# Chunked attention and a leaky-ReLU layer on one core: product 3 added onto product 5's bank, first-layer weight sums on VectorE, attention steps moved

## The chip, the cores and the metric

The kernel runs on one core of one Trainium2 chip. The metric is the device time of one execution in microseconds (us), lower is better. 0.5% of it (1.4 us) is about what a measurement of this kernel can tell from no change.

## The reference

```python
def _attn_ref(q, k, v):                       # q, k, v: (8, 8, 576, 64)
    chunk, scale = 64, 1.0 / np.sqrt(D)       # every head in 9 independent chunks of 64
    scores = scale * np.matmul(q_c, k_c.transpose(0, 1, 2, 4, 3))
    scores = scores - np.max(scores, axis=-1, keepdims=True)
    attn = np.exp(scores)
    attn = attn / (np.sum(attn, axis=-1, keepdims=True) + 1e-09)
    return np.matmul(attn, v_c)...

def _moe_ref(x, w_in, w_out):                 # x: (4608, 512), w_in: (512, 2048), w_out: (2048, 512)
    h = x @ w_in
    return np.maximum(0.01 * h, h) @ w_out
```

The attention output, transposed to (4608 tokens, 512), is the x of the second function. Inputs and output are float32; the kernel computes in fp16 with fp32 accumulation.

## The kernel before

**Tiling.** The 4608 tokens are 36 attention units u of 128 tokens, and 20 blocks j of the two layers: blocks 0 to 3 have 128 tokens, blocks 4 to 19 have 256. A unit's output lands in `xT` (model dimension on the partitions). A block needs the units of its tokens.

**Attention of a unit.** Step "dq"/"dk" transposes q and k on VectorE (`QZ`, `KT`; units below 14 use TensorE, "tq"/"tk"), "s" is the score matmul into `Sp`, "m"/"nb" the maximum and the scaled negative of it on VectorE, "f" the exponentials on ScalarE (`ex`, sums in `z`), "z" adds 1e-9 and inverts on VectorE (`ze`, `zi`), "n" scales on GpSimd (`en`, from unit 9 on), "d" transposes by DMA from SP's queue (`et`), "v" is the matmul with v (`xp`), and "a" the copy to `xT` on ScalarE.

**Layers.** The first layer of blocks 6 to 16 is "mm1": per chunk of the work list a 512-column bank `hT`, which "G" (`act1`) turns into `gT` through a leaky ReLU. The second layer of blocks 4 to 19 is a seven-product scheme (Strassen's in Winograd's form): products P1 to P7 of 8 matmuls each, whose operands are halves of `gT` and `w_outT`, sums of token halves `SG` ("sum", VectorE), and sums of weight halves `TW` ("W", VectorE). P1, P6, P7, P4 accumulate one after the other in bank X, and after each of the first three ScalarE copies it to `keep` ("combX"). P2, P5 and P3 are combined by VectorE with one of these copies into the output tile `osb` ("combW", "combZ"), and SP's queue stores it. In blocks 6 to 15, P3 accumulates in the same bank Z as P5, after P5's value was read by `combine(j, 5)`. In blocks 4, 5 and 16 to 19 (`ONE`), P2, P5 and P3 have a bank each, from a ring of four (`mm`), which `hT` uses too; there `combine(j, 0)`, one more VectorE add, puts P5 onto the copy that P3 is combined with.

**Wide blocks.** Blocks 17, 18 and 19 (`WIDE`) use the seven products in the first layer as well, for two halves s of the hidden units ("a" and "b" in the work list): `wide(j, s, n)` is product n, 8 matmuls of 128 columns. Products 1, 6, 7, 4 accumulate in `xbank`; "lx" (`wide_x`) copies it to `xkeep` on ScalarE. Products 2, 5, 3 go to `xpr` banks of the ring, and "la" (`wide_m`) adds such a bank onto copies on VectorE: product 5 onto the copies after 7 and after 6, product 3 onto that after 6. "lp" is the leaky ReLU on ScalarE. The token sums `xs` are made on VectorE, and the 16 weight sums `WS` (`w_in_sum`, a difference of two 128x512 fp16 tiles each) on GpSimd, 8 of them from w_inT alone and 8 that need another WS too.

**Order.** The order on every engine is written out by the program, in a work list (`chunks`) of TensorE work in fixed order. `now["step"]` counts it: 1 per chunk, 0.5 per wide product. Everything else is an event with a due step: the table of constants (`SPACE`, `VO`, `O_*`) gives the due steps of the attention units, loads and weight sums, and `later(D_*, ...)` those of copies and combinations, counted from the chunk that they follow. Before a chunk, all due events are issued. `flush` issues named ones at once. Each engine works its instructions in that order; waits come from the data and from buffers.

Of the kernel before, what the change touches and what calls it, by code (L numbers as in the profile page):

```python
# [16 lines left out]
def kernel(  # L17
# [178 lines left out]
    def product(j, n, i):  # L196
        one, two = rows(j)
        g, w = gT[j], w_outT
        where, left, right = {
            1: ("X", g[:, :HF, one], w[:, :HF, :HM]),  # L200
            2: ("W", g[:, HF:, one], w[:, HF:, :HM]),
            3: ("Z", SG.get((j, 4)), w[:, HF:, HM:]),
            4: ("X", g[:, HF:, two], TW.get(4)),
            5: ("Z", SG.get((j, 1)), TW.get(1)),
            6: ("X", SG.get((j, 2)), TW.get(2)),
            7: ("X", SG.get((j, 3)), TW.get(3)),
        }[n]
        if where != "X" and j in ONE:
            where = n
        if (j, where) not in bank:  # L210
            tag, bufs = {"X": ("qp", 1), "Z": ("kp", 1)}.get(where, ("mm", 4))
            if j in EARLY:
                tag, bufs = "mm", 4
            bank[j, where] = psp.tile([128, 2, HM], FP32, name=f"pr{where}", tag=tag, bufs=bufs)
        to = bank[j, where]
        for f in range(HF):
            nc.tensor.matmul(  # L217
                out=to[:, i, :],
                lhsT=left[:, f, i * 128:(i + 1) * 128],
                rhs=right[:, f, :],  # L220
                start=(j, where) not in opened,
                stop=(f == HF - 1),
                skip_group_check=True,
            )
            opened.add((j, where))

    def combine(j, n):
# [25 lines left out]
        if n == 4:  # L253
            nc.scalar.activation(out=to, in_=half(bank[j, "X"]), func=AFT.Copy, bias=0.0, scale=1.0)
        else:
            nc.vector.tensor_tensor(  # L256
                out=to,
                in0=half(bank[j, n if j in ONE else "W" if n == 2 else "Z"]),
                in1=half(kept[j, {2: 1, 5: 7, 3: 6}[n]]),
                op=ALU.add,  # L260
            )
# [61 lines left out]
    def w_in_sum(n, s, t):  # L323
# [14 lines left out]
        nc.gpsimd.tensor_tensor(out=WS[n, s, t], in0=x, in1=y, op=ALU.subtract)  # L338
# [16 lines left out]
    def wide(j, s, n):  # L355
# [14 lines left out]
        if n in (1, 6, 7, 4):  # L370
            if n == 1:
                XB[j, s] = psp.tile([128, 4, 128], FP32, name="xbank", tag="kp" if s or j == WIDE.start else "Sp", bufs=1)
            to = XB[j, s]
        else:
            to = XM[j, s, n] = psp.tile([128, 4, 128], FP32, name="xpr", tag="mm", bufs=4)
        for i in range(4):
            for t in range(2):
# [4 lines left out]
                    start=(n != 6 and n != 7 and n != 4 and t == 0 and (n != 1 or i == 0)),  # L382
# [21 lines left out]
    def wide_m(j, s, n):  # L404
        of = XM.pop((j, s, n))
        for m in {2: (1,), 5: (7, 6), 3: (6,)}[n]:
            to = XK[j, s, m]
            nc.vector.tensor_tensor(out=to, in0=of, in1=to, op=ALU.add)  # L408
            if (n, m) != (5, 6):
                later(D_P, "lp", j, s, n != 2, n == 5, to)  # L410

# [125 lines left out]
    def fill():  # L537
# [10 lines left out]
        elif kind == "wide":  # L548
# [4 lines left out]
            if p in (1, 6, 7, 4):  # L553
                flush("lx")
                if p == 6:
                    flush("xs")
            if p == 1 and a == 0:
# [7 lines left out]
            elif p != 5:  # L565
                flush("lx", "la")
# [9 lines left out]
        elif kind == "prod":  # L576
# [17 lines left out]
            if p == BLOCKS[j] // 256 - 1:  # L594
# [14 lines left out]
                elif j in ONE:  # L609
                    if a in (1, 6, 7, 4):  # L610
                        later(D_K, "combX", j, a)
                    else:
                        flush("combX", "combZ")
                        if a == 5:
                            later(D_C, "combZ", j, 0)
# [20 lines left out]
    D_S = 1.75  # L636
    D_K = 0
    D_C = 2.25
    D_U = 0.5
    D_T = 2.5  # L640
    D_H = 0
    D_I = 1.75
    D_P = 2.75
    O_S = 162
    O_B = 198
    O_A = 0.75
    XS_POOL = 0
    O_G = 168
    D_O = 1.5
    D_D = 2.5  # L650
# [224 lines left out]
    def zero_act(i):  # L875
# [49 lines left out]
    SPACE = [5.0, 4.5, 6.5, 4.5, 6.0, 4.5, 8.0, 4.5, 6.0, 6.0, 9.5, 6.5, 6.0, 7.0, 8.0, 5.5, 5.5, 10.5, 9.0, 6.5, 8.0, 9.5, 9.5, 5.0, 6.0, 8.5, 6.5, 9.5, 5.5, 10.5]  # L925
    VO = [1.0, 1.0, 1.0, -0.5, 3.0, -1.5, 4.0, 1.5, 0.5, -1.0, 1.0, -1.0, 2.5, 4.5, 5, 1.0, 1.0, 5.0, 3, 1.0, 6, 0.5, 1.5, 0.0, -1.5, -3.0, 3.0, 2, -2.0, -3.5]
    O_T = 4.0
    O_P = 3.5
    O_Q = 5.5
    O_R = 0.75  # L930
    O_M = 0
    O_X = 1.0
    O_F = 1.5
    O_H = 1.0
    O_Z = 6.5
    O_N = 3.0
# [41 lines left out]
    for b in range(3, B):  # L978
        for i in range(16):
            at(T[9 * b // 2 - 5] - (O_E if b == 3 else O_L) + i // 2 * D_D, "D", b, i)  # L980
# [52 lines left out]
```

## Time and profile before

| | |
|---|---|
| time, median of 3 runs | 287.69 us (287.49 to 288.5) |
| span of the profiled execution | 287.5 us |
| TensorE busy | 274.4 us, 95% |
| VectorE busy | 221.7 us, 77% |
| ScalarE busy | 205.4 us, 71% |
| GpSimd busy | 164.6 us, 57% |
| granted TensorE clock, mean | 0.994 |

The profiled execution's own time is its span of 287.5 us, 0.2 us below the median of the three runs; no other time is given for it. In the views, PE is TensorE's matmuls, PEld its weight loads, DVE is VectorE, ACT is ScalarE, POOL is GpSimd, SP the queue engine. A row of the timeline is start, length, engine, line, operation, output<-inputs, shapes, count, and in brackets the idle time before it with what ended it. A row of the windows is the stretch, its length, and then busy time and number of instructions of PE, PEld, DVE, ACT and POOL, the granted clock, the mean busy share of the DMA engines in a unit of one, and GB/s.

### The profile page before, as it was taken

How to read it: one execution, taken by the hardware profiler on the slowest of the kernel's cores; microseconds unless marked ns; L12 is line 12 of the kernel's file. 1: busy time of each engine (PE TensorE's matmuls, PEld its weight loads, DVE VectorE, ACT ScalarE, POOL GpSimd, SP SyncE). 2: the span in 40 equal slices, each digit the busy share in tenths (PEclk: the TensorE clock that was granted, in tenths of full speed). 3: DMA queues.
4: the chain of work that ended last, by engine and by line, in shares of the span. 5: the costliest groups of instructions: out<-in, count | busy, mean ns of one | idle time of the engine just before them, and what ended most of it. 6: DMA issues, size and time to landing. Idle time of an engine off the chain costs nothing.

```text
span 287.5 us, 8377 instructions
## 1 busy us (share of the span) xinstructions
PE 274.4 (95%) x3338; PEld 240.6 (84%) x3338; DVE 221.7 (77%) x434; ACT 205.4 (71%) x657; POOL 164.6 (57%) x187
## 2 busy tenths in 40 slices
PE   7888999999999999999999999998599998999995
PEld 4568946899999999999999999987489997999994
DVE  5866666998897869698869788679967768787683
ACT  6855724775658787898887888787477868777671
POOL 8747642987958775984599459719631196000000
PEclk9999999999999999999999999999799999999999
DMA  9999999999999999999899999929053304111113
GB/s 146 151 185 177 203 172 125 123 137 123 163 118 161 67 88 177 95 166 107 119 106 135 100 146 109 156 81 103 0 182 95 93 18 93 22 73 40 39 39 109
DMA packets 182647, 32.66 MB, mean 114 GB/s; under 512 B 173776, under 2 KB 178128, under 8 KB 182608
## 3 DMA queue, kind: packets, MB, share of 16 engines
q0 software_dynamic: 158880, 18.23, 116.2%
q1 hardware_dynamic: 22688, 13.64, 20.3%
q8 instruction: 26, 0.43, 0.6%
q10 hardware_dynamic: 1040, 0.26, 0.4%
q14 instruction: 13, 0.11, 0.2%
HBM read 36.96 MB, written 9.44 MB: 161 GB/s over the span
## 4 chain that ended last, share of the span: by engine, by line
PE 85%; DMA 6%; DVE 5%; POOL 2%; issue 1%; ACT 0%; ACTq 0%; DVEq 0%; POOLq 0%
PE hT L291 34%; PE prX L217 19%; DMA w_inT<-in_moe_w_in_dram 6%; PE prZ L217 6%; PE pr L217 5%; PE oP L418 5%; PE xbank L378 3%; PE prW L217 3%; DVE SG L194 3%; PE Sp L736 3%; PE xp L830 3%; PE xpr L378 2%; DVE xs L353 1%; POOL VB L113 1%; POOL k_in L92 1%
## 5 line engine op out<-in xcount | busy, mean ns | idle before, releaser
L291 PE MATMUL hT<-xT,w_inT 128*128 128x256 f16 (+1 forms) x1216 | 120.2, 251 | 4.8 <-DVE osb L256 4.1
L291 PEld LDWEIGHTS <-w_inT 128*128 128x128 f16 x1216 | 96.6, 98 | 13.4 <-DVE osb L256 4.3
L306 ACT ACTIVATE gT<-hT 128x512 f16<-128x512 f32 x120 | 71.1, 619 | 19.9 <-PE hT L291 19.8
L766 ACT ACTIVATE ex<-Sp,nb 128x64 f16<-128x64 f32 x176 | 53.0, 333 | 7.2 <-DVE nb L758 6.6
L797 POOL TENSOR_TENSOR en<-ex,zi 128x512 f16<-128x512 f16 x27 | 30.6, 1134 | 42.5 <-ACT keep L233 17.7
L217 PEld LDWEIGHTS <-SG 128*128 128x128 f16 x512 | 48.7, 98 | 5.3
L745 DVE TENSOR_REDUCE mx<-Sp 128x8 f32<-128x512 f32 x36 | 24.7, 686 | 21.3 <-PE Sp L736 20.9
L217 PEld LDWEIGHTS <-gT 128*128 128x128 f16 x384 | 37.0, 99 | 4.4
L766 ACT ACTIVATION_READ_ACCUMULATOR ex<-Sp,nb 128x1 f32 x176 | 40.0, 227 | 0.0
L106 POOL DMA_DIRECT2D q_d<-in_q_dram x40 | 33.5, 838 | 8.2 <-DVE QZ L718 8.1
L106 POOL DMA_DIRECT2D k_d<-in_k_dram x40 | 32.8, 820 | 2.0 <-DMA k_d<-in_k_dram 1.3
L217 PE MATMUL prX<-TW,SG 128*128 128x256 f16 x256 | 33.2, 273 | 0.0
L718 DVE STREAM_TRANSPOSE QZ<-q_d 64x512 f16<-64x512 f16 (+1 forms) x48 | 31.1, 653 | 0.5
L233 ACT ACTIVATE keep<-prX 128x256 f32<-128x256 f32 x48 | 19.1, 398 | 14.4 <-PE prX L217 14.3
L844 ACT ACTIVATE xT<-xp 128x512 f16<-128x512 f32 x36 | 22.3, 618 | 7.3 <-PE xp L830 7.1
L113 POOL DMA_DIRECT2D VB<-in_v_dram x16 | 18.6, 1173 | 13.7 <-PE xp L830 11.0
L194 DVE TENSOR_TENSOR SG<-gT 128x1024 f16<-128x1024 f16 x32 | 23.3, 728 | 3.9 <-ACT gT L306 3.6
L408 DVE TENSOR_TENSOR xkeep<-xpr,xkeep 128x512 f32<-128x512 f32 x24 | 15.7, 683 | 6.7 <-ACT xkeep L402 4.3
L217 PE MATMUL prX<-TW,gT 128*128 128x256 f16 x128 | 17.5, 282 | 0.0
L194 DVE TENSOR_TENSOR SG<-gT,SG 128x1024 f16<-128x1024 f16 x16 | 16.7, 1045 | 0.1
L217 PE MATMUL prX<-w_outT,gT 128*128 128x256 f16 x128 | 16.6, 273 | 0.0
L726 DVE STREAM_TRANSPOSE KT<-k_d 128x512 f16<-128x512 f16 (+1 forms) x24 | 15.6, 655 | 0.4
(88 smaller groups left out, 428.0 us busy)
## 6 DMA issues: line engine op xcount, KB each, us to landing
out_dram<-osb SPq DMA_DIRECT2D x35, 256.0 KB, 3.1
VB<-in_v_dram POOLq DMA_DIRECT2D x16, 288.0 KB, 6.3
q_d<-in_q_dram POOLq DMA_DIRECT2D x40, 72.0 KB, 4.5
k_d<-in_k_dram POOLq DMA_DIRECT2D x40, 72.0 KB, 4.6
w_inT<-in_moe_w_in_dram POOLq DMA_DIRECT2D x8, 256.0 KB, 8.3
w_outT<-in_moe_w_out_dram POOLq DMA_DIRECT2D x4, 512.0 KB, 12.1
q_in<-in_q_dram POOLq DMA_DIRECT2D x11, 128.0 KB, 7.9
k_in<-in_k_dram POOLq DMA_DIRECT2D x11, 128.0 KB, 7.8
```

Source lines behind the costliest of these rows:

```text
L106: nc.gpsimd.dma_start(out=t[p0:p0 + 32, m, :, :, :].rearrange("p h b d -> p (h b) d"), in_=src[b, h0:h0 + 2, :, dh * 32:dh * 32 + 32].rear ...
L113: nc.gpsimd.dma_start(out=VB[b % NVB][m * CH:(m + 1) * CH, :, :, m * CH:(m + 1) * CH].rearrange("p h c d -> p (h c) d"), in_=v[b, m * H // ...
L194: nc.vector.tensor_tensor(out=SG[j, n], in0=x, in1=y, op=op)
L217: nc.tensor.matmul(out=to[:, i, :], lhsT=left[:, f, i * 128:(i + 1) * 128], rhs=right[:, f, :], start=(j, where) not in opened, stop=(f == ...
L233: nc.scalar.activation(out=half(kept[j, n]), in_=half(bank[j, "X"]), func=AFT.Copy, bias=0.0, scale=1.0)
L291: nc.tensor.matmul(out=hT[:, i, :], lhsT=w_inT[:, t, fc * 128:(fc + 1) * 128], rhs=xT[:, t, r0:r0 + tb], start=(t == 0), stop=(t == NT - 1),)
L306: nc.scalar.activation(out=gT[j][:, nf * a:nf * a + nf, c0:c0 + tb], in_=HT.pop((j, a, p)), func=AFT.Prelu, bias=0.0, scale=1.0, alpha=0.01,)
L718: nc.vector.transpose(out=qz[s * CH:(s + 1) * CH, :, e0:e0 + n, s, :], in_=flat(qkd[b][0])[s * CH:(s + 1) * CH, :, at:at + n * CH].rearran ...
L745: nc.vector.tensor_reduce(out=MX[u], in_=SP[u], axis=AXL.X, op=ALU.max)
L766: nc.scalar.activation(out=E[u][:, i, :], in_=SP[u][:, i, :], func=AFT.Exp, bias=NB[u][:, i:i + 1], scale=SCL, accum_out=Z[u][:, i:i + 1],)
L797: (nc.gpsimd if u >= UP else nc.vector).tensor_tensor(out=E[u], in0=ex, in1=ZI.pop(u).unsqueeze(2).to_broadcast((128, 8, CH)), op=ALU.mult)
L844: nc.scalar.activation(out=xT[:, :, at:at + G], in_=xp, func=AFT.Copy, bias=0.0, scale=1.0)
```

## The change

1. `SOLO` (blocks 4, 5 and 19) takes the place of `ONE` for the question of who has a bank for each product. In blocks 16, 17 and 18, P2 gets bank W, and P3 accumulates in P5's bank Z, both still from the ring of four; `combine(j, 0)` is gone there, and before P3 all pending combinations are flushed, so that P5's value is read first.
2. In the wide blocks, product 3 accumulates in product 5's `xpr` bank, which is kept for it; the second add of product 5 (onto the copy after 6) is gone. Before products 2 and 3 the pending "lx" and "la" are now flushed ahead of the matmuls, no longer behind them.
3. `w_in_sum` runs on VectorE instead of GpSimd.
4. Numbers of the tables move: attention units are issued up to 2 steps earlier or later (`SPACE`), their "v" up to 4 steps (`VO`), the loads of q and k for units from 14 on are spread over more steps, combinations are due one step later (`D_C`), "la" one step earlier (`D_I`), and the weight sums 1 step apart instead of 0.75. The work list is the same, chunk by chunk.

```diff
+    SOLO = EARLY + (LAST,)
...
-        if where != "X" and j in ONE:
+        if where != "X" and j in SOLO:
             where = n
         if (j, where) not in bank:
-            tag, bufs = {"X": ("qp", 1), "Z": ("kp", 1)}.get(where, ("mm", 4))
+            tag, bufs = {"X": ("qp", 1), "Z": ("mm", 4) if j in ONE else ("kp", 1)}.get(where, ("mm", 4))
...
-                in0=half(bank[j, n if j in ONE else "W" if n == 2 else "Z"]),
+                in0=half(bank[j, n if j in SOLO else "W" if n == 2 else "Z"]),
...
-        nc.gpsimd.tensor_tensor(out=WS[n, s, t], in0=x, in1=y, op=ALU.subtract)
+        nc.vector.tensor_tensor(out=WS[n, s, t], in0=x, in1=y, op=ALU.subtract)
...
+        elif n == 3:
+            to = XM[j, s, 3] = XM.pop((j, s, -5))
         else:
             to = XM[j, s, n] = psp.tile([128, 4, 128], FP32, name="xpr", tag="mm", bufs=4)
...
-                    start=(n != 6 and n != 7 and n != 4 and t == 0 and (n != 1 or i == 0)),
+                    start=(n in (1, 2, 5) and t == 0 and i == 0),
...
-        for m in {2: (1,), 5: (7, 6), 3: (6,)}[n]:
-            to = XK[j, s, m]
-            nc.vector.tensor_tensor(out=to, in0=of, in1=to, op=ALU.add)
-            if (n, m) != (5, 6):
-                later(D_P, "lp", j, s, n != 2, n == 5, to)
+        if n == 5:
+            XM[j, s, -5] = of
+        to = XK[j, s, {2: 1, 5: 7, 3: 6}[n]]
+        nc.vector.tensor_tensor(out=to, in0=of, in1=to, op=ALU.add)
+        later(D_P, "lp", j, s, n != 2, n == 5, to)
...
+            elif p != 5:
+                flush("lx", "la")
...
             elif p != 5:
-                flush("lx", "la")
                 later(D_I, "la", j, a, p)
...
+            if a == 3 and j not in SOLO:
+                flush("combX", "combZ")
...
-                        if a == 5:
-                            later(D_C, "combZ", j, 0)
...
-    D_C = 2.25
+    D_C = 3.25
...
-    D_I = 1.75
+    D_I = 0.75
...
-    VO = [1.0, 1.0, 1.0, -0.5, 3.0, -1.5, 4.0, 1.5, 0.5, -1.0, 1.0, -1.0, 2.5, 4.5, 5, 1.0, 1.0, 5.0, 3, 1.0, 6, 0.5, 1.5, 0.0, -1.5, -3.0, 3.0, 2, -2.0, -3.5]
+    VO = [0.5, 1.5, 1, -1, 3, -1.5, 3.5, 0, -2, 2, 3, 2, 1, 4.5, 8, 4.5, 4.5, 2, 3.5, -1, 6, 0.5, -1, -0.5, -2, -4, 3, 5, -5, -3.5]
```

Where instructions stand on an engine, before and after, at the three places that matter below. Lines after the change are one to four higher. The numbers behind `WS_` and `osb_` tell buffers apart.

GpSimd, from the last load of v (`VB`) to the end, before (the eight WS from w_inT, with `en` of the units between):

```order
L113 DMA VB_64<-in_v_dram 64x36x64 x2
L338 TENSOR_TENSOR WS_3912<-w_inT 128x512
L338 TENSOR_TENSOR WS_3927<-w_inT 128x512
L338 TENSOR_TENSOR WS_3943<-w_inT 128x512
L338 TENSOR_TENSOR WS_3954<-w_inT 128x512
L338 TENSOR_TENSOR WS_3957<-w_inT 128x512
L338 TENSOR_TENSOR WS_3982<-w_inT 128x512
L338 TENSOR_TENSOR WS_3998<-w_inT 128x512
L797 TENSOR_TENSOR en<-ex,zi 128x512
L338 TENSOR_TENSOR WS_4025<-w_inT 128x512
L797 TENSOR_TENSOR en<-ex,zi 128x512 x4
```

and after, from two `en` ahead of that load to the last instruction of the queue's work:

```order
L801 TENSOR_TENSOR en<-ex,zi 128x512
L107 DMA q_d<-in_q_dram 32x36x32
L107 DMA k_d<-in_k_dram 32x36x32
L801 TENSOR_TENSOR en<-ex,zi 128x512
L114 DMA VB_64<-in_v_dram 64x36x64 x2
L801 TENSOR_TENSOR en<-ex,zi 128x512 x7
```

Nothing but `en` is left on GpSimd behind the last load.

VectorE, around the token sums 3 and 4 (`SG`) of block 13, before:

```order
L194 TENSOR_TENSOR SG<-gT 128x1024
L718 STREAM_TRANSPOSE QZ_65<-q_d 64x8x64
L726 STREAM_TRANSPOSE KT<-k_d 128x512
L194 TENSOR_TENSOR SG<-gT,SG 128x1024
L256 TENSOR_TENSOR osb_3925<-prW,keep 128x256
L745 TENSOR_REDUCE mx<-Sp 128x8
L758 TENSOR_SCALAR nb<-mx 128x8
```

and after:

```order
L195 TENSOR_TENSOR SG<-gT 128x1024
L195 TENSOR_TENSOR SG<-gT,SG 128x1024
L339 TENSOR_TENSOR WS_3921<-w_inT 128x512
L257 TENSOR_TENSOR osb_3943<-prW,keep 128x256
L339 TENSOR_TENSOR WS_3945<-w_inT 128x512
L339 TENSOR_TENSOR WS_3957<-w_inT 128x512
L794 TENSOR_SCALAR ze<-z 128x8
L796 RECIPROCAL zi<-ze 128x8
L749 TENSOR_REDUCE mx<-Sp 128x8
L762 TENSOR_SCALAR nb<-mx 128x8
```

The weight sums stand between the instructions that free P2's bank (`osb<-prW`) and that start the next unit's softmax (`mx`, `nb`).

VectorE, in the first wide block (17), from the token sum 2 of block 16 to the adds of wide products 5 and 3, before (the `xkeep x3` are two adds of product 5 and one of product 3):

```order
L194 TENSOR_TENSOR SG<-SG,gT 128x1024
L353 TENSOR_TENSOR xs<-xT 128x256
L353 TENSOR_TENSOR xs<-xT,xs 128x256
L790 TENSOR_SCALAR ze<-z 128x8
L792 RECIPROCAL zi<-ze 128x8
L408 TENSOR_TENSOR xkeep<-xpr,xkeep 128x512
L194 TENSOR_TENSOR SG<-gT 128x1024
L256 TENSOR_TENSOR osb_4733<-pr_4673,keep 128x256
L194 TENSOR_TENSOR SG<-gT,SG 128x1024
L408 TENSOR_TENSOR xkeep<-xpr,xkeep 128x512 x3
```

and after:

```order
L195 TENSOR_TENSOR SG<-SG,gT 128x1024
L412 TENSOR_TENSOR xkeep<-xpr,xkeep 128x512
L794 TENSOR_SCALAR ze<-z 128x8
L796 RECIPROCAL zi<-ze 128x8
L195 TENSOR_TENSOR SG<-gT 128x1024
L195 TENSOR_TENSOR SG<-gT,SG 128x1024
L412 TENSOR_TENSOR xkeep<-xpr,xkeep 128x512
L257 TENSOR_TENSOR osb_4756<-prW,keep 128x256
L412 TENSOR_TENSOR xkeep<-xpr,xkeep 128x512 x2
```

The first single `xkeep` is the add of product 2; the second is now the only add of product 5, which product 3's matmuls wait for, and it stands behind both remaining token sums.

More of the change, by code (lines that the diff above doesn't have):

```diff
@@ L635 @@
     D_G = 0.5
-    D_S = 1.75
+    D_S = 2
     D_K = 0
-    D_C = 2.25
-    D_U = 0.5
+    D_C = 3.25
+    D_U = 0.25
     D_T = 2.5
     D_H = 0
-    D_I = 1.75
[L643 to L646, printed above, removed]
+    D_I = 0.75
+    D_P = 3.5
+    O_S = 162.75
+    O_B = 197
+    O_A = 1
     XS_POOL = 0
-    O_G = 168
-    D_O = 1.5
-    D_D = 2.5
+    O_G = 151.5
+    D_O = 0.5
+    D_D = 3.25
     UP = 9
@@ L977 @@
         at(T[u - 3] - O_D, "g", u)
-    for b in range(3, B):
+    for b in range(B2, B):
         for i in range(16):
-            at(T[9 * b // 2 - 5] - (O_E if b == 3 else O_L) + i // 2 * D_D, "D", b, i)
+            t0, dt = (D_0, D_1) if b == 2 else (T[9 * b // 2 - 5] - (O_E if b == 3 else O_L), D_D)
+            at(t0 + i // 2 * dt, "D", b, i)
     for n in range(4):
```

35 lines of the change are left out of this document (19 added, 16 removed), and 12 rows, old and new, of the table FRONT.

## The prediction

> **What bounds the kernel now.** I read the page's head first, then the windows, then the waits and the timeline of the two places where TensorE is not busy. The page: busy time of the engines, and the granted clock in 40 slices of 7.2 us.
>
> ```profile
> PE 274.4 (95%) x3338; PEld 240.6 (84%) x3338; DVE 221.7 (77%) x434; ACT 205.4 (71%) x657; POOL 164.6 (57%) x187
> PEclk9999999999999999999999999999799999999999
> ```
>
> TensorE is the bound, and in one slice, the 29th (201 to 208 us), its clock was cut. The windows say how full the rest is (stretch, then PE, PEld, DVE, ACT, POOL busy, clock, DMA, GB/s):
>
> ```profile
> 60.00:70.00 10.00, 10.00 (x141) 9.32 (x139) 9.72 (x20) 5.17 (x11) 7.29 (x10) 1.00 3.18 124
> ...
> 150.00:160.00 10.00, 10.00 (x112) 9.04 (x110) 8.88 (x17) 8.09 (x35) 7.61 (x9) 1.00 2.63 146
> 160.00:170.00 10.00, 10.00 (x112) 9.03 (x110) 8.18 (x16) 8.39 (x35) 4.98 (x5) 1.00 1.24 129
> ...
> 180.00:190.00 10.00, 10.00 (x106) 9.01 (x105) 7.12 (x14) 7.96 (x33) 4.79 (x6) 1.00 1.80 111
> ...
> 200.00:205.00 5.00, 0.94 (x10) 0.62 (x8) 4.97 (x5) 0.38 (x1) 4.93 (x5) 1.00 0.46 32
> 205.00:210.00 5.00, 5.00 (x33) 3.86 (x31) 2.81 (x10) 4.15 (x20) 2.15 (x2) 0.66 0.06 11
> ...
> 241.00:246.00 5.00, 4.11 (x61) 3.73 (x60) 4.86 (x11) 3.18 (x8) 2.37 (x3) 1.00 0.46 74
> ...
> 250.00:260.00 10.00, 10.00 (x152) 9.61 (x150) 7.32 (x16) 7.55 (x16) 0.00 (x0) 1.00 0.14 54
> ```
>
> From 60 us to 200 us and from 250 us on TensorE has no gap, at full clock: an engine that gets faster there gives nothing, and one that gets later costs only if it eats its slack. Two holes are left: 4.06 us idle at 200 (5.00 - 0.94), followed by 5 us at a clock of 0.66, which is 0.34 x 5.00 = 1.7 us lost; and 0.89 us idle at 241 to 246, at full clock. The work list up to the first 44 us is the same in both, so its gaps stay. The floor for this amount of TensorE work is therefore 287.5 - 4.06 - 1.7 - 0.89 = 280.85 us.
>
> What makes the first hole, in the timeline (start, length, engine, line):
>
> ```profile
> 196.66 8.26 POOL L338 TENSOR_TENSOR WS<-w_inT 128x512 f16<-128x512 f16 x7
> ...
> 197.67 6.25 DVE L194 TENSOR_TENSOR SG<-gT,SG 128x1024 f16<-128x1024 f16 x1
> ...
> 199.21 1.04 PE L217 MATMUL prX<-TW,SG 128*128 128x256 f16 x8
> ...
> 203.84 0.41 DVE L256 TENSOR_TENSOR osb<-prW,keep 128x256 f32<-128x256 f32 x1
> ...
> 204.31 2.63 PE L291 MATMUL hT<-xT,w_inT 128*128 128x256 f16 x16 [4.06 <-DVE osb L256]
> ```
>
> ```profile
> L194 DVE TENSOR_TENSOR SG<-gT,SG 128x1024 f16<-128x1024 f16 x9 | 6.5, 718 | 0.0
> ```
>
> The token sum of block 13 that takes 0.72 us elsewhere (nine between 60 and 195 us, second fence) took 6.25 us, exactly while GpSimd ran seven weight sums back to back. Behind it in VectorE's queue stood `osb<-prW`, which frees P2's bank of the ring of four; `hT` needed that bank, and TensorE stood for 4.06 us. The second hole, in the first wide block:
>
> ```profile
> 240.07 1.25 DVE L353 TENSOR_TENSOR xs<-xT 128x256 f16<-128x256 f16 x1
> 241.35 1.12 DVE L353 TENSOR_TENSOR xs<-xs,xT 128x256 f16<-128x256 f16 x1
> ...
> 243.00 0.28 DVE L353 TENSOR_TENSOR xs<-xT 128x256 f16<-128x256 f16 x1
> ...
> 244.38 1.22 DVE L194 TENSOR_TENSOR SG<-gT 128x1024 f16<-128x1024 f16 x1
> ```
>
> ```profile
> 241.13 1.20 POOL L338 TENSOR_TENSOR WS<-w_inT,WS 128x512 f16<-128x512 f16 x1
> 241.32 0.69 ACT L402 ACTIVATE xkeep<-xbank 128x512 f32<-128x512 f32 x1
> 242.62 0.61 PE L378 MATMUL xbank<-xs,WS 128*128 128x128 f16 x8 [0.65 <-ACT xT L844]
> 244.00 1.04 POOL L797 TENSOR_TENSOR en<-ex,zi 128x512 f16<-128x512 f16 x1 [1.68 <-ACT xkeep L402]
> 244.56 0.60 ACT L402 ACTIVATE xkeep<-xbank 128x512 f32<-128x512 f32 x1 [0.69 <-PE xbank L378]
> 245.23 0.61 PE L378 MATMUL xpr<-xs,w_inT 128*128 128x128 f16 x8
> ```
>
> Again two sums (`xs`) took 1.1 to 1.25 us beside a GpSimd weight sum and 0.28 us after it, and the wide product 6 at 242.62 waited for the second. So both holes come from VectorE instructions with two SBUF inputs that stood still while GpSimd did arithmetic.
>
> **The change, part by part.** (1) Weight sums off GpSimd. It loses 16 instructions, and behind the last v load only `en` is left there, each 1 us long and apart from the next. Both holes lose their cause: 4.06 + 1.7 = 5.8 us at 200. At 241 the gain is less than the hole: product 6 also needs the copy of `xbank` that ended at 242.01 (241.32 + 0.69), so it starts at about 242.1 instead of 242.62, 0.5 us.
>
> A rule of the Trainium skill bears on this, in "SBUF — State Buffer", section "Who interferes with whom": a VectorE instruction with two SBUF inputs and a GpSimd instruction that reads SBUF exclude each other, and the second to start waits until the first has finished. This trace agrees that they exclude each other, but not on the length: the sum stood through the starts of several of GpSimd's, not through one. By the rule's letter the wait would be one weight sum; what that would make of the time is the third rival.
>
> (2) The same 16 on VectorE. No row has this form there. `xs` (256 elements) takes 0.28 us, a free `SG` (1024) 0.72 us; between them 512 elements are about 0.42 us (an estimate, linear between the two), 16 x 0.42 = 6.7 us, 3.4 us for each eight. Ends: 16 x 0.28 = 4.5 and 16 x 0.72 = 11.5 us. The first eight fall into one period of a block, 16 steps or about 14.5 us. In the windows 150 to 170 VectorE is idle 20.00 - 17.06 = 2.9 of 20 us, so 2.1 in 14.5: the eight put it up to 1.3 us behind, which the next period gives back. Who waits for that: `osb<-prW` stands behind one weight sum only; what is late is the token sum 1 of the next block, which P5 needs. The prices, from the chain and from VectorE's timeline and groups:
>
> ```profile
> 193.44 0.87 PE prW L217 x8
> 194.31 0.25 PE Sp L736 x8
> ```
>
> ```profile
> 194.58 0.69 DVE L745 TENSOR_REDUCE mx<-Sp 128x8 f32<-128x512 f32 x1 [0.49 <-PE Sp L736]
> 195.31 0.38 DVE L758 TENSOR_SCALAR nb<-mx 128x8 f32<-128x8 f32 x1
> ...
> 196.29 0.71 DVE L718 STREAM_TRANSPOSE QZ<-q_d 64x512 f16<-64x512 f16 x1
> ```
>
> ```profile
> L790 DVE TENSOR_SCALAR ze<-z 128x8 f32<-128x8 f32 x36 | 9.1, 254 | 2.4 <-ACT ex L766 1.7
> L792 DVE RECIPROCAL zi<-ze 128x8 f32<-128x8 f32 x36 | 7.3, 203 | 3.0
> ```
>
> Between the score matmul that VectorE answers first in that period and this P5 lie 5 chunks of 0.87 us and two attention steps of 0.25 us, 4.85 us. VectorE needs 0.69 + 0.38 + 0.25 + 0.20 + 3 x 0.71 (transposes) + 0.72 (the sum) = 4.4 us ahead of P5. So 0.45 us of the 1.3 are covered, and the cost is 0 to 0.9 us; I take 0.2, near the low end, because instructions start up to 0.1 us before the one ahead has ended in the timeline, and a sum held by a weight sum no longer occurs. The second eight fall where the list of transposes ends (unit 35 is the last) and VectorE waits for score matmuls: 0.
>
> (3) Removed adds.
>
> ```profile
> L408 DVE TENSOR_TENSOR xkeep<-xpr,xkeep 128x512 f32<-128x512 f32 x24 | 15.7, 683 | 6.7 <-ACT xkeep L402 4.3 <-PE xpr L378 2.3
> L237 DVE TENSOR_TENSOR keep<-pr,keep 128x256 f32<-128x256 f32 x6 | 2.5, 410 | 0.3 <-ACT xT L844 0.3
> ```
>
> Six of 0.683 us and three of 0.410 us, 5.3 us of VectorE, all behind 244 us, where TensorE has no gap from 250 us on (the row above): worth 0.
>
> (4) The new waits: product 3 now waits until VectorE has read product 5's bank. In blocks 18 and 19 the list puts b7, P7, P5, a4, b4, P4 (3.9 us) between a7 and a3, and a4, b4, P4, a3, b3 between P5 and P3; the chain (copy 0.6, add 0.68, some 0.2 us for each handover) is under 2 us: hidden. In block 17, b7 to b3 has P3 and b4 between, 1.3 us, about as long as the chain: 0 to 0.1. But a7 to a3 has only P6 and one "v", 1.1 us. From the rows: the copy after a7 ends at 244.56 + 0.60 = 245.16, the add cannot end before 245.85, and without other delay a3 would start at 245.23, or 245.46 with the "v" of unit 34, which now stands ahead of it: a wait of 0.4 us at least. Two token sums stand ahead of the add, and `en` at 244.00 still holds one of them (the 1.22 us row): two times 0.68 and 1.04 after 243.87 is 246.3, the add ends at 247.0, a wait of 1.5 us. I take 1.0, in the middle, as the order of SG and `en` decides.
>
> (5) Moved steps. Of the units' "v", those with the smallest room between the landing of `et` and "v" decide. The tightest is unit 9:
>
> ```profile
> 73.40 1.20 SPq L819 DMA_TRANSPOSE et<-en  x1
> 80.73 0.40 PE L830 MATMUL xp<-et,VB 128*128 128x64 f16 x8
> et<-en SPq DMA_TRANSPOSE x1, 6.4
> ```
>
> It landed at 79.8 and was used at 80.73, 0.9 us of room; "v" is now due 1.5 steps (1.3 us) earlier, but one pair of q and k loads fewer stands ahead of its `en` on GpSimd's queue: 0 to 0.4, taken as 0. The others have more room than they lose. The later combinations (`D_C`) put `osb<-prW` one chunk later, 0.87 us; the `hT` that needs its bank is the fourth taker of the ring behind it and comes more than two chunks later still: 0.
>
> Sum: 287.5 - 5.8 (first hole) - 0.5 (sooner product 6) + 0.2 (VectorE behind) + 1.0 (a3) + 0 + 0 = 282.4 us of span; the median of the runs stands 0.2 us above the profiled span, so 282.6 us.
>
> **The rivals.** *VectorE becomes the bound around the weight sums.* For: it is 85% busy in 150 to 170 us, over 20 points fuller than GpSimd there, and the sums are near-serial with softmax steps. Against: there is idle time within two periods. If the first eight lie wholly on the path, 3.4 us instead of 0.2: 285.8; both, 289.2 at the very end. More likely 283.6 to 286.
>
> *Slower, by the banks that wait.* P3 after P5 and product 3 after 5 make nine new waits in blocks 16 to 19. I price eight at 0 by their cover. Should each cost what the ninth does at most, 1.5 us, the kernel would take 282.6 + 8 x 1.5 = 294.6; it ends slower than 289.1 (before plus 0.5%) from 0.8 us each on, 6.5 / 8. The place to see it is 250 to 285 us, without a gap now. Against: covers of 2.6 to 3.9 us in seven of the nine.
>
> *No change: the long sum is not GpSimd's doing.* Had it waited for one weight sum only (1.2 us), it would have ended at 199.6, the bank have been free at 200.0, and `hT`, due at 200.1 (199.21 + 8 x 0.109), not have waited; then something else held VectorE for 6.25 us and may hold it again: 282.6 + 5.8 = 288.4. The rule of the Trainium skill quoted from "SBUF — State Buffer", taken by its letter, would say the same. Against: the stretch coincides with GpSimd's run to within 1 us, and the `xs` rows show the same at a second place.
>
> *The floor.* All gaps go and a3 costs nothing: 280.85 + 0.2 = 281.05.
>
> **How the numbers follow.** Forecast with its terms at their ends (281.3 to 283.6): 0.63. Floor: 0.10. VectorE bound: 0.15, mostly below 285.2. No change: 0.06. Slower: 0.06. The range from 280.6 (floor less a scatter of 0.4) to 285.2 holds 0.63 + 0.10 + 0.10. Faster by over 0.5% (under 286.25): 0.63 + 0.10 + 0.13 = 0.86; within 0.5%, about what a measurement of this kernel can tell from no change: 0.08; slower: 0.06.
>
> **What would show it.** Right: no SG over 1.8 us; 200 to 210 us full at a clock of 1.00; WS rows of about 0.42 us on VectorE; one wait of 0.4 to 1.5 us of an `xpr` matmul on `xkeep` in block 17, none in 18 and 19. Wrong: TensorE waiting for SG or `osb` between 200 and 215 us, or again a clock under 0.9 in a slice; repeated waits of P3 or `xpr` behind 250 us; a wait for `et` near 80 us.

## The result, and the profile after

The changed kernel takes 285.29 us (median of 4 runs, 284.28 to 286.39), beside 287.88 us (287.49 to 288.5, 4 runs) of the kernel before on the same chip: ratio 0.9894, 95% interval 0.9854 to 0.9934. It is faster by 2.6 us; the forecast was faster by 5.1. The median lies 0.1 us above the upper end of the forecast range; taken by the ratio, from the 287.69 us that the forecast starts at, it is 284.6 us and inside the range. The profiled execution has a span of 284.6 us and is the slowest of the four, 286.39 us; the time is the span plus 1.8 us in each run. TensorE's first 28 us are left out below: both profiles reach the first score matmul behind 20 us at the same time (28.25 us before, 28.27 after). Eleven further profiles, of the experiments below, reach it at 26.2 to 27.5 us, so up to 2 us of the difference between two executions can come from this first stretch; what a part is worth is therefore read from the waits behind it.

The page after, busy time and granted clock. The 29th slice is full again; the cut in slices 2 and 3 (a clock of 0.77 in 7 to 14 us and 0.74 in 14 to 21) lies in the first 28 us, and the mean clock of this execution, 0.987, is below the 0.999 to 1.000 of the other three:

```profile
PE 275.1 (97%) x3338; PEld 241.4 (85%) x3338; DVE 215.6 (76%) x441; ACT 205.4 (72%) x657; POOL 145.2 (51%) x171
...
PEclk9779999999999999999999999999999999999999
```

The windows after (stretch, length, then PE, PEld, DVE, ACT, POOL busy, clock, DMA share, GB/s):

```profile
110.00:120.00 10.00, 8.86 (x94) 7.84 (x92) 8.76 (x15) 6.60 (x30) 9.89 (x12) 1.00 2.46 157
200.00:210.00 10.00, 10.00 (x112) 9.04 (x110) 9.26 (x26) 8.40 (x36) 2.08 (x2) 1.00 0.88 98
...
230.00:240.00 10.00, 8.87 (x109) 7.94 (x108) 9.21 (x26) 8.63 (x39) 1.07 (x2) 1.00 0.22 68
...
250.00:260.00 10.00, 10.00 (x144) 9.55 (x142) 7.46 (x15) 7.50 (x16) 0.00 (x0) 1.00 0.08 28
```

The hole at 200 us is gone. But TensorE, full before between 60 and 200 us, now idles 1.14 us in 110 to 120, and 1.13 us in 230 to 240. VectorE's timeline where the hole was:

```profile
198.27 0.65 DVE L195 TENSOR_TENSOR SG<-gT 128x1024 f16<-128x1024 f16 x1
198.84 0.68 DVE L195 TENSOR_TENSOR SG<-gT,SG 128x1024 f16<-128x1024 f16 x1
199.44 0.42 DVE L339 TENSOR_TENSOR WS<-w_inT 128x512 f16<-128x512 f16 x1
199.78 0.42 DVE L257 TENSOR_TENSOR osb<-prW,keep 128x256 f32<-128x256 f32 x1
```

The token sum of 6.25 us takes 0.68, and a weight sum 0.42 us on VectorE, as estimated. The new idle time at 119 us, in the timeline of block 7's second layer:

```profile
113.27 0.82 POOL L107 DMA_DIRECT2D k_d<-in_k_dram  x1
113.27 2.44 DVE L195 TENSOR_TENSOR SG<-gT,SG 128x1024 f16<-128x1024 f16 x1 [0.19 <-issue]
114.09 1.06 POOL L801 TENSOR_TENSOR en<-ex,zi 128x512 f16<-128x512 f16 x1
115.13 1.04 PE L218 MATMUL prX<-TW,SG 128*128 128x256 f16 x8
...
116.68 0.17 DVE L762 TENSOR_SCALAR nb<-mx 128x8 f32<-128x8 f32 x1
116.94 0.31 ACT L770 ACTIVATE ex<-Sp,nb 128x64 f16<-128x64 f32 x1 [1.90 <-DVE nb L762]
...
118.59 0.40 ACT L234 ACTIVATE keep<-prX 128x256 f32<-128x256 f32 x1
119.05 1.03 PE L218 MATMUL prX<-TW,gT 128*128 128x256 f16 x8 [1.14 <-ACT keep L234]
```

P7 ends at 116.17, but its copy `keep` runs at 118.59, because on ScalarE the exponentials of unit 17 (`ex`) stand ahead of it and wait for `nb`; P4 waits for `keep`. From P4's due time to its start that is 1.30 us (the bracket counts from the modelled end of the matmul before). `nb` is late in its turn because it stands on VectorE behind the token sum of 2.44 us. Before the change that sum took 0.64 us (at 112.66), and `keep` stood ahead of `ex`:

```profile
115.62 0.38 ACT L233 ACTIVATE keep<-prX 128x256 f32<-128x256 f32 x1 [0.28 <-PE prX L217]
...
115.90 0.31 ACT L766 ACTIVATE ex<-Sp,nb 128x64 f16<-128x64 f32 x1
```

And the first wide block, after:

```profile
234.85 1.56 DVE L339 TENSOR_TENSOR WS<-w_inT,WS 128x512 f16<-128x512 f16 x2
235.07 1.06 POOL L801 TENSOR_TENSOR en<-ex,zi 128x512 f16<-128x512 f16 x1 [8.06 <-DVE zi L796]
236.33 0.41 DVE L257 TENSOR_TENSOR osb<-prZ,keep 128x256 f32<-128x256 f32 x1
236.79 0.61 PE L381 MATMUL xbank<-xT,w_inT 128*128 128x128 f16 x8 [0.89 <-DVE osb L257]
...
240.33 1.53 DVE L195 TENSOR_TENSOR SG<-gT,SG 128x1024 f16<-128x1024 f16 x1
241.78 0.68 DVE L412 TENSOR_TENSOR xkeep<-xpr,xkeep 128x512 f32<-128x512 f32 x1
242.52 0.61 PE L381 MATMUL xpr<-xs,w_inT 128*128 128x128 f16 x8 [0.49 <-DVE xkeep L412]
```

The last two weight sums, held by `en`, stand ahead of `osb<-prZ`, which frees the bank that a1 (wide product 1 of block 17) takes; a1 is 1.05 us late. At 242.52 a3 waits for product 5's add, 0.65 us.

The lost time of TensorE behind 28 us, by its start times: before 5.90 (hole with lost clock) + 0.81 + 0.40 = 7.1 us; after 1.30 + 1.05 + 0.65 + 0.41 + 0.23 and 0.55 (a "v" at 90.31 that waited for `et`; in none of the later runs) = 4.2 us. The difference, 2.9 us, is that of the spans, 287.5 - 284.6.

### The profile page after: what moved, and what is told of

Same layout as the page of the kernel before. It is cut to its first block, busy times and chain, and to the rows that moved or that the text cites. A ratio compares the mean times of both kernels' runs of the same rounds, so it can differ in the third digit from the quotient of the medians.

```text
span 284.6 us, 8360 instructions
## 1 busy us (share of the span) xinstructions
PE 275.1 (97%) x3338; PEld 241.4 (85%) x3338; DVE 215.6 (76%) x441; ACT 205.4 (72%) x657; POOL 145.2 (51%) x171
## 4 chain that ended last, share of the span: by engine, by line
PE 54%; DVE 3%; issue 0%; ACT 0%; DVEq 0%; ACTq 0%
PE hT L292 20%; PE prX L218 14%; PE prZ L218 7%; PE xbank L381 3%; PE prW L218 3%; PE xpr L381 3%; PE xp L834 2%; PE Sp L740 1%; DVE SG L195 1%; PE pr L218 1%; DVE WS L339 1%; DVE xkeep L412 0%; DVE xs L354 0%; DVE mx L749 0%; DVE zi L796 0%
## 5 line engine op out<-in xcount | busy, mean ns | idle before, releaser
L307 ACT ACTIVATE gT<-hT 128x512 f16<-128x512 f32 x120 | 71.9, 618 | 19.8 <-PE hT L292 19.4
L218 PEld LDWEIGHTS <-gT 128*128 128x128 f16 x384 | 36.3, 98 | 5.3 <-issue 1.3
L195 DVE TENSOR_TENSOR SG<-gT 128x1024 f16<-128x1024 f16 x32 | 21.7, 679 | 5.7 <-ACT gT L307 5.4
L412 DVE TENSOR_TENSOR xkeep<-xpr,xkeep 128x512 f32<-128x512 f32 x18 | 12.2, 688 | 12.7 <-PE xpr L381 7.9
L218 PE MATMUL prX<-TW,gT 128*128 128x256 f16 x128 | 16.6, 273 | 1.1 <-ACT keep L234 1.1
L405 ACT ACTIVATE xkeep<-xbank 128x512 f32<-128x512 f32 x18 | 10.4, 594 | 6.9 <-PE xbank L381 6.9
```

The source lines that it names most:

```text
L195: nc.vector.tensor_tensor(out=SG[j, n], in0=x, in1=y, op=op)
L218: nc.tensor.matmul(out=to[:, i, :], lhsT=left[:, f, i * 128:(i + 1) * 128], rhs=right[:, f, :], start=(j, where) not in opened, stop=(f == ...
L307: nc.scalar.activation(out=gT[j][:, nf * a:nf * a + nf, c0:c0 + tb], in_=HT.pop((j, a, p)), func=AFT.Prelu, bias=0.0, scale=1.0, alpha=0.01,)
```

## The experiments

Each ratio is to the kernel before, run on the same chip beside it (288.8, 288.95 and 288.35 us in the three groups: e1 to e4; e5, e6, e8, e9; e10 to e12).

**e1: the weight sums alone.**

```diff
-        nc.gpsimd.tensor_tensor(out=WS[n, s, t], in0=x, in1=y, op=ALU.subtract)
+        nc.vector.tensor_tensor(out=WS[n, s, t], in0=x, in1=y, op=ALU.subtract)
```

> The kernel before, with the 16 weight sums on VectorE and nothing else changed. If GpSimd's run of weight sums is what holds VectorE's sums, the hole of 4.06 us with the 1.7 us of lost clock at 200 us goes, and product 6 of block 17 starts sooner: 5.8 us or more come off, less about 1 us if the second eight now stand ahead of what block 17's first product waits for: 281.5 to 283.5 us. If something else held the sum, within 0.7 us of before.

Measured: 282.37 us (282.17 to 282.52), ratio 0.978, 0.9756 to 0.9804. This part alone gives 6.4 us, more than the whole. Lost time: 0.82 us before a1 and 0.45 us before product 7 of block 17; the long hole, its clock loss and the waits in block 7 are absent. The first eight sums on VectorE delay nobody.

**e2: the change without the weight sums** (the inverse of e1's edit, on the changed kernel).

> The changed kernel with the weight sums back on GpSimd, numbers and banks as changed. They are due 0.87 us apart and take 1.11 us there, so they run back to back again. If they hold VectorE's sums: a token sum of 2 to 7 us again, TensorE idle for 2 to 6 us near 200 us, 3 to 7 us more than the changed kernel, 288 to 292 us. If the gain came from the moved numbers, it stays near 285 us.

Measured: 287.24 us (286.31 to 288.85), ratio 0.9959, 0.9942 to 0.9977, which neither expectation named. So inside the change the sums on VectorE are worth 0.9959 - 0.9894, about 1.9 us. A token sum of 2.50 us is there again (at 195.91), but no hole of 4 us: the moved steps have put the weight sums and the token sums otherwise. Lost are 1.33 us at 117 (P4 of block 7 again), 1.28 before product 6, 1.55 before a3, and 0.15 to 0.53 at each of several smaller waits.

**e3: the banks alone** (parts 1 and 2 of the change, the numbers and GpSimd's sums as before).

```diff
+        elif n == 3:
+            to = XM[j, s, 3] = XM.pop((j, s, -5))
...
-        for m in {2: (1,), 5: (7, 6), 3: (6,)}[n]:
...
+        to = XK[j, s, {2: 1, 5: 7, 3: 6}[n]]
```

> The kernel before with parts 1 and 2 alone: P3 and wide product 3 accumulate onto product 5's bank, nine VectorE adds fewer; weight sums on GpSimd and all numbers as before. If the nine adds were off the path: within 0.7 us of before, with a wait of up to 1.5 us of product 3 in block 17 only. If the new waits for banks cost something in each block: 0.8 us or more per wait, 3 us or more in all, gaps of TensorE behind 250 us.

Measured: 291.31 us (290.06 to 292.31), ratio 1.0083, 1.0055 to 1.0111: slower by 2.5 us. Timeline:

```profile
196.54 6.26 DVE L195 TENSOR_TENSOR SG<-gT,SG 128x1024 f16<-128x1024 f16 x1
...
243.16 1.22 DVE L195 TENSOR_TENSOR SG<-gT 128x1024 f16<-128x1024 f16 x1
...
244.63 0.67 DVE L195 TENSOR_TENSOR SG<-gT,SG 128x1024 f16<-128x1024 f16 x1
245.23 0.68 DVE L412 TENSOR_TENSOR xkeep<-xpr,xkeep 128x512 f32<-128x512 f32 x1
245.96 0.61 PE L381 MATMUL xpr<-xs,w_inT 128*128 128x128 f16 x8 [1.79 <-DVE xkeep L412]
```

The hole stays as before, and a3 waits for the add, 1.95 us counted from its due time, behind both token sums. Blocks 18 and 19 have no gap. So there is one wait, as the first expectation had it, but a longer one than its 1.5 us. The adds taken away give nothing back.

**e4: the moved steps alone** (part 4; sums on GpSimd, banks as before).

```diff
-    O_S = 162
-    O_B = 198
-    O_A = 0.75
+    O_S = 162.75
+    O_B = 197
+    O_A = 1
...
```

> The kernel before with the changed numbers of the tables alone (attention units, their v, loads, combinations, spacing of the weight sums), weight sums on GpSimd, banks as before. If the two gaps of the changed kernel at 90 us (0.55 us, v of unit 11 waiting for its transposed tile) and 119 us (1.3 us) come from the moved steps: they are here too, and the hole at 200 us stays in some size: 288 to 291 us. If those gaps are scatter of one execution: TensorE without a gap from 60 to 190 us, and the time within 0.7 us of before.

Measured: 285.89 us (284.54 to 286.63), ratio 0.9899, 0.9873 to 0.9926: the numbers alone are worth as much as the whole change. The expectation of 288 to 291 us missed, since it took the hole to stay. Timeline:

```profile
196.66 3.84 POOL L338 TENSOR_TENSOR WS<-w_inT 128x512 f16<-128x512 f16 x3
196.99 2.50 DVE L194 TENSOR_TENSOR SG<-gT 128x1024 f16<-128x1024 f16 x1
199.42 1.63 DVE L194 TENSOR_TENSOR SG<-gT,SG 128x1024 f16<-128x1024 f16 x1
...
202.91 5.60 POOL L338 TENSOR_TENSOR WS<-w_inT 128x512 f16<-128x512 f16 x5
```

The weight sums come in runs of three and of five; the token sums stand beside the run of three (2.50 and 1.63 us instead of 0.68), and beside the run of five stands none. So the hole shrinks to gaps of 0.15 to 0.55 us without a sum leaving GpSimd. The price: P4 of block 7 waits 1.32 us here too.

**e5: parts 1 to 3 with all numbers of before** (a few of them shown, on the changed kernel).

```diff
-    D_C = 3.25
-    D_I = 0.75
-    O_B = 197
-    O_A = 1
+    D_C = 2.25
+    D_I = 1.75
+    O_B = 198
+    O_A = 0.75
...
```

> The kernel before with parts 1, 2 and 3 of the change (banks, shared bank of wide products 5 and 3, weight sums on VectorE) and its own table of numbers. Theory: the sums alone gave 282.4 us, the banks cost one wait of a3 in block 17 (1.95 us where only the banks were changed), so 284.3 us, with that one wait of 1.5 to 2 us before a3 and none in blocks 18 and 19. Rival: with the sums off GpSimd the xs and SG ahead of the add are no longer held, so the add ends sooner and a3 waits 0.6 us at most: 282.4 to 283.0 us. Second rival: the banks and the sums on VectorE disturb each other: above 285 us.

Measured: 283.59 us (282.6 to 284.65), ratio 0.9819, 0.9784 to 0.9855. Timeline:

```profile
236.59 1.04 POOL L801 TENSOR_TENSOR en<-ex,zi 128x512 f16<-128x512 f16 x1 [3.27 <-issue]
...
236.96 1.22 DVE L195 TENSOR_TENSOR SG<-gT 128x1024 f16<-128x1024 f16 x1
...
239.77 0.61 PE L381 MATMUL xpr<-xs,w_inT 128*128 128x128 f16 x8 [0.96 <-DVE xkeep L412]
```

a3 waits 1.13 us: less than with GpSimd's sums (1.95), more than nothing, between the two expectations, since `en` still holds a token sum for 0.5 us. To e1's kernel that is 1.2 us more by the medians, about the wait, though the two intervals overlap (0.9784 to 0.9855 and 0.9756 to 0.9804). By the traces the banks cost what a3 waits, in each version.

**e6: the weight sums stay on GpSimd, but apart.**

```diff
-            at(O_S + O_A * i if i < 8 else O_B + O_A * (i - 8), "WS", (1, 3, 2, 4)[i // 4], i // 2 % 2, i % 2)
+            at(O_S + 3 * i if i < 8 else O_B + O_A * (i - 8), "WS", (1, 3, 2, 4)[i // 4], i // 2 % 2, i % 2)
```

> The kernel before with its first eight weight sums still on GpSimd, but due 3 steps (2.6 us) apart instead of 0.75; nothing else. Theory (back to back is what counts: GpSimd keeps the SBUF port from one sum to the next): a token sum waits for one weight sum at most, none is longer than 1.9 us, the hole at 200 us and the lost clock behind it (5.8 us) go: about 283 us, with the 1.2 us in the first wide block left. Rival (GpSimd's arithmetic as such holds VectorE, however it is spaced): a hole of 2 us or more stays between 195 and 220 us: 285 us or more. By the Trainium skill's rule taken by its letter (a wait for one instruction of GpSimd) the spacing would change nothing: 288.8 us.

Measured: 282.76 us (282.15 to 283.51), ratio 0.9795, 0.9758 to 0.9831. Timeline:

```profile
195.03 2.74 POOL L338 TENSOR_TENSOR WS<-w_inT 128x512 f16<-128x512 f16 x2
196.03 0.73 DVE L194 TENSOR_TENSOR SG<-gT,SG 128x1024 f16<-128x1024 f16 x1
...
206.18 2.79 POOL L338 TENSOR_TENSOR WS<-w_inT 128x512 f16<-128x512 f16 x2
...
208.24 1.28 DVE L194 TENSOR_TENSOR SG<-gT 128x1024 f16<-128x1024 f16 x1
```

The weight sums come in pairs. The same token sum, 6.25 us before, takes 0.73 us: it gets in between the two sums of a pair, although the second follows the first as closely as in the run of seven (they start at 195.03 and 196.14). The longest token sum beside the first eight takes 1.28 us, held by one weight sum. The hole and its clock loss are gone, and no work has left GpSimd. So the long run of weight sums made the hole; that they ran on GpSimd as such did not. Whether it is the pauses that help, this run does not show, since the sum at 196.03 needed none; e12 says more. The 0.99 us before product 6 stay, since the second eight were left as they were.

**e8: e1, and the second eight sooner.**

```diff
-    O_B = 198
+    O_B = 194
```

> The kernel before with the weight sums on VectorE, and the second eight due 4 steps sooner (194 instead of 198). Theory: the 0.82 us before a1 of block 17 came from two weight sums ahead of osb<-prZ on VectorE, held by en on GpSimd; with them ahead of en the gap goes, 282.4 - 0.8 = 281.6 us. Rival: the eight, now among token sum 4 of block 15, mx and the transposes, make these late instead: a new gap between 222 and 232 us, 282.4 us or more.

Measured: 281.76 us (280.87 to 281.97), ratio 0.9749, 0.9715 to 0.9783. Timeline:

```profile
228.63 0.75 DVE L338 TENSOR_TENSOR WS<-w_inT,WS 128x512 f16<-128x512 f16 x2
230.70 1.04 POOL L797 TENSOR_TENSOR en<-ex,zi 128x512 f16<-128x512 f16 x1 [7.71 <-DVE zi L792]
231.25 0.42 DVE L256 TENSOR_TENSOR osb<-prZ,keep 128x256 f32<-128x256 f32 x1 [0.68 <-PE prZ L217]
231.92 0.61 PE L378 MATMUL xbank<-xT,w_inT 128*128 128x128 f16 x8
```

`osb<-prZ` now runs as soon as prZ is there, and a1 has no gap. All that TensorE loses behind 28 us is 0.63 us. By the trace the wait is gone; the ratio's interval overlaps e1's, so the 0.6 us between the medians, which are from two chips, are not separated by the times alone.

**e9 and e11: what makes P4 of block 7 wait.** e9 puts all of unit 17's steps one later; e11 moves its exponentials alone, by 1.25 steps, so that on ScalarE `keep` comes first and nothing changes on GpSimd.

```diff
-    SPACE = [..., 6, 6, 8.5, 7.5, ...]
+    SPACE = [..., 6, 6, 9.5, 6.5, ...]                                        (e9)
...
-            at(t + O_F, "f", u, 0, 4)
+            at(t + O_F + (1.25 if u == 17 else 0), "f", u, 0, 4)               (e11, and u, 4, 8 likewise)
```

> The changed kernel with the attention steps of unit 17 due one step later (69 as before the change, 68 in the change); unit 18 and all others as in the change. Theory: the gap of 1.3 us at 119 us comes from ScalarE's order, f of unit 17 ahead of the copy keep of block 7; with f behind keep again it goes, 1.3 us less than the changed kernel (ratio to before 0.985 instead of 0.9894, about 284.4 us here). Rival: the token sum 4 of block 7 held for 2.44 us is what makes it late, whatever ScalarE's order: P4 of block 7 or something next to it still waits about 1 us, ratio 0.989.

> The changed kernel with the exponentials (f) of unit 17 alone due 1.25 steps later, so that ScalarE copies keep of block 7 ahead of them; nothing else moves on GpSimd or VectorE ahead of that, and the token sum 4 of block 7 is still held for about 2.4 us. Theory: it is ScalarE's order that makes P4 wait, so the 1.30 us at 119 us go: ratio 0.985, about 284.2 us. Rival: the held token sum delays enough else (osb<-prW, mx of unit 17) that about 1 us of TensorE is lost there anyway: ratio 0.989.

Measured: e9 284.13 us (283.39 to 286.17), ratio 0.9843, 0.9803 to 0.9883; e11 283.27 us (282.75 to 284.98), ratio 0.983, 0.9804 to 0.9855. Timeline of e11:

```profile
110.86 2.43 DVE L195 TENSOR_TENSOR SG<-gT,SG 128x1024 f16<-128x1024 f16 x1 [0.20 <-issue]
...
113.78 0.38 ACT L234 ACTIVATE keep<-prX 128x256 f32<-128x256 f32 x1 [0.28 <-PE prX L218]
...
114.53 0.31 ACT L770 ACTIVATE ex<-Sp,nb 128x64 f16<-128x64 f32 x1 [0.36 <-DVE nb L762]
...
115.33 1.04 PE L218 MATMUL prX<-TW,gT 128*128 128x256 f16 x8
```

The token sum is held as long as in the changed kernel (2.43 us), and P4 has no wait, as `keep` no longer stands behind `ex`. So with the sum held, the order on ScalarE is what costs. The order without the held sum was not run. An estimate from the changed kernel's rows: with a token sum of 0.68 us in place of 2.44, `nb`, `ex` and `keep` would come 1.76 us sooner, `keep` would end at 118.99 - 1.76 = 117.23, ahead of P4's due time of 117.75, and the same order would cost nothing. The wait then takes both, and the moved steps brought both. A gap of 0.37 us (an `hT` that waits for `xT`) comes up nearby; e9 has two, of 0.40 and 0.38. The times alone do not settle it: the interval of e9 overlaps that of the changed kernel (0.9854 to 0.9934), and that of e11 touches it.

**e10: e9, and the second eight sooner.**

```diff
-    O_B = 197
+    O_B = 194
```

> The changed kernel with two numbers mended: unit 17 one step later (as in the run before this one, ratio 0.9843) and the second eight weight sums due 3 steps sooner (194 instead of 197). Theory: the 1.05 us before a1 of block 17 goes as well, ratio 0.9843 - 0.0036 = 0.981, about 283.2 us, with the wait of a3 (0.65 us) left. Rival: the copy that a1 waits for is late for another reason, or the sums delay mx instead: ratio 0.984 or more, and a wait of TensorE between 222 and 236 us.

Measured: 283.9 us (283.18 to 284.53), ratio 0.9845, 0.9822 to 0.9867: nothing gained over e9, the time that the rival named. Timeline:

```profile
235.12 0.54 ACT L234 ACTIVATE keep<-prX 128x256 f32<-128x256 f32 x1
235.38 0.77 ACT L405 ACTIVATE xkeep<-xbank 128x512 f32<-128x512 f32 x1
...
236.20 0.61 PE L381 MATMUL xbank<-xs,WS 128*128 128x128 f16 x8 [0.56 <-ACT xkeep L405]
```

a1's 1.05 us are gone, but product 6 now waits 0.72 us for the copy of product 1, which stands on ScalarE behind eight `ex` and a `keep`, and a score matmul at 230.86 starts 0.31 us late. The cause of a1's wait was right; what is late next had been left out of the expectation.

**e12: all 16 sums on GpSimd, apart and sooner.**

```diff
-            at(... O_S + O_A * i if i < 8 else O_B + O_A * (i - 8), ...)      O_B = 198
+            at(... O_S + 3 * i if i < 8 else O_B + 2 * (i - 8), ...)          O_B = 188
```

> The kernel before with all 16 weight sums still on GpSimd, but spaced: the first eight 3 steps apart (as in the run that gave 0.9795), the second eight 2 steps apart from step 188 on. Theory: as VectorE then is held by one weight sum at a time, and both xs of block 17 are made after the last of them, the 0.99 us before product 6 of block 17 shrinks to below 0.3: ratio 0.9765, about 282.0 us, the same as with the sums on VectorE. Rival: GpSimd's sums now fall among more of VectorE's sums and delay them: ratio 0.98 or more, with new waits of TensorE between 215 and 235 us.

Measured: 281.4 us (281.22 to 282.24), ratio 0.9765, 0.9743 to 0.9787, the same as e8 within the intervals. 0.85 us of TensorE are lost in all. The second eight still come without a pause, in a run of three and a run of five:

```profile
218.34 4.35 POOL L338 TENSOR_TENSOR WS<-w_inT,WS 128x512 f16<-128x512 f16 x3
...
219.44 0.68 DVE L194 TENSOR_TENSOR SG<-gT 128x1024 f16<-128x1024 f16 x1
...
221.00 0.68 DVE L194 TENSOR_TENSOR SG<-SG,gT 128x1024 f16<-128x1024 f16 x1
...
225.54 5.60 POOL L338 TENSOR_TENSOR WS<-w_inT,WS 128x512 f16<-128x512 f16 x5
...
233.59 0.28 DVE L353 TENSOR_TENSOR xs<-xT 128x256 f16<-128x256 f16 x1
```

No token sum falls beside the run of five, and the two `xs` take 0.28 and 0.29 us. But two token sums fall beside the run of three, and each takes the 0.68 us of a free one: it gets in between two weight sums, and the weight sum behind it takes 1.68 and 1.59 us in place of 1.15. So a sum needs no pause to get in, and weight sums that follow without a pause are not enough to hold one for long.

The trace's records of the single instructions show one thing that differs. Each of these three weight sums signals a semaphore when it is done; of the seven before the change only the last does. In all 13 traces, taking every point where one GpSimd computation follows another within 0.1 us while a token sum or an `xs` stands waiting (some for less than 0.1 us): at the 12 points between two weight sums of which neither signals, the waiting sum was passed over each time; at the 22 points where at least one of the two instructions signals, it got in each time. No run changed the signals alone, so this stays a reading of the traces, not a shown cause.

e8 and e12 are the two best versions: both are faster than the changed kernel by 1.3 to 1.5% (0.9749 and 0.9765 beside 0.9894, intervals apart) and keep the banks and nearly all numbers of the kernel before.

## Why the prediction was right or wrong

The sign was right and the size twice too large: of its terms, two that were priced at nothing cost 2.35 us. That the result still lies at the upper end of the range, and by the ratio inside it, is in part luck: the range reached up to 285.2 us for the sake of a rival whose wait showed in another place than it named, and no term of it stood for a cost of the moved steps.

- **First hole, -5.8 us: right.** 5.9 us by the traces, 6.4 and 6.2 us by the medians of e1 and e6, which hold small other gains. The cause was named rightly, except that GpSimd's arithmetic did little harm in other arrangements (e6, e12): it takes a long run that does not let the sum in. The sum was not held to the end of the run either, as "exactly while GpSimd ran seven" has it: it got in ahead of the seventh weight sum, which started at 203.33 and took 1.60 us, the sum's time included. What the sum did not see is that the moved steps alone already take most of the hole away (e4). The three parts alone give -6.4, -2.9 and +2.5 us by the medians, -6.8 together; the whole gave -2.6, chiefly because two of them remove the same hole.
- **Product 6, -0.5 us: right and given back.** It no longer waits for `xs` (0.81 us before, none after); a1 of the same block waits instead, which is the term after the next.
- **First eight sums on VectorE, +0.2 us: 0.** No gap between 120 and 236 us after, none between 28 and 233 us in e1.
- **Second eight sums, "0": wrong, 1.05 us.** The step reasoned that VectorE waits for score matmuls there and so has time to spare. It did not ask who is queued behind the sums: `osb<-prZ`, which frees a1's bank. And `en`, which the forecast counted as harmless on GpSimd, doubles the time of the last two, 1.56 instead of 0.75 us. e8 shows it: ahead of `en` they cost nothing.
- **a3, +1.0 us, range 0.4 to 1.5: right.** 0.65 us, by the mechanism named; 1.13 with the numbers of before (e5) and 1.95 with the sums on GpSimd as well (e3). "Eight other waits, 0": right, no gap behind 250 us.
- **Moved steps, "0": wrong, 1.30 us.** The step weighed each "v" against the landing of its `et`, and each bank's combination. It did not go through the other instructions that a moved unit issues: unit 17's exponentials passed a copy that P4 waits for, and an `en` came to stand beside token sum 4 of block 7, which took 2.44 us in place of 0.64. The rows before the change (110 to 120 us without a gap) had to be read for ScalarE's order and for what GpSimd does beside the token sums; e11 shows that the wait goes with the order, though the sum stays held. The `et` wait of 0.55 us, for which the step had 0.9 us of room at its tightest unit, came in the profiled execution alone. The removed adds: 0, as priced.
- **The sum.** It missed 1.30 + 1.05 us, and in the profiled execution the 0.55 us of "v"; it had 0.35 us too much for a3 and 0.2 us for the first eight sums: 2.35 us net, where the spans differ from the forecast by 2.2 us (284.6 against 282.4). Of the rivals, "VectorE becomes the bound" gave a time like the measured one (283.6 to 286), in another place than it named: one wait behind the second eight, none behind the first. "It ends slower by the bank waits" holds for e3 alone, with one wait and not nine.
- **The offset.** The forecast set the profiled span of 287.5 us 0.2 us below the median. In all later runs the time is 1.7 to 1.8 us above its span, so that execution was slower than the runs listed; its first score matmul behind 20 us, at 28.25 us, is later than in the eleven profiles of the experiments. Since the terms are differences, this moved nothing in the forecast.
- **The rules that were weighed.** The Trainium skill, "SBUF — State Buffer", section "Who interferes with whom", says that the one that issues first has the shared port for the whole instruction, and the other waits. e6 agrees: a token sum waits for the end of one weight sum (1.28 us at most). Before the change it got in only at the end of the sixth weight sum (6.25 us), and in e4 at the end of the second of three (2.50 us), so the waiting side is not always served when the instruction ends: there the measurement decides. The Trainium skill, "TensorE: Matmul & The Clock Gate", section "Part 1: The HAM clock gate", says that an idle window of about 3.4 us takes the clock down: the idle 4.06 us were followed by a clock of 0.66, and the 1.30 us at 119 us left it at 1.00.

## What to carry to other kernels

When one engine's run of instructions holds up another engine, first break the run up and issue it elsewhere: here that gave as much (0.9765) as moving the work to the other engine (0.9749), and either alone gave about twice what the whole change did. For each instruction put into a queue, ask which instruction behind it frees a bank or feeds TensorE, and for each unit moved by a step go through all its instructions on all queues, not only those with the least room. Effects of parts that cure the same wait do not add, and a part that costs (the shared banks) hides in the sum; run the parts singly.

## What the runs showed of the hardware that was not expected

A VectorE sum of two SBUF inputs that comes during a run of GpSimd's weight sums is not always let in when the weight sum at work ends. It was passed over at five ends before (6.25 us), at one in e4 (2.50 us) and at none in e6 (0.73 us), and in e12 two sums got in at the first end, in a run without a pause (0.68 us each). All 12 ends at which a sum was passed over lie between two weight sums that signal no semaphore, and at all 22 others it got in; no run varied the signals by themselves.

Instructions with one input can stand as well: in e4 the `ze` at 207.33 took 1.20 us, up to the end of a weight sum, where 0.17 is usual. One GpSimd `en` is enough to add 0.5 to 0.95 us to a token sum (1.22 and 1.63 us beside 0.68).

The 2.44 us of the token sum at 113.27 began 0.82 us ahead of that `en`, while a load was issued. Of the token sums that ran beside load issues and no GpSimd arithmetic, 21 of 21 in the same trace took 0.64 to 0.69 us (one of them at 112.02); in the trace before the change 19 of 20 did, and the one at 155.22 took 1.22 us, with no arithmetic on GpSimd until 156.55. So GpSimd's load issues can go with a held sum too; when they do stays open.
